# FFN tiles of 432 tokens for the last three batches, and a last output tile in three parts, in an attention + ReGLU kernel

## The chip, the cores and the metric

One core of a Trainium2 chip. The metric is the device time of one execution in microseconds. A verdict compares runs of the two kernels made on the same chip. "Ratio" is the mean time of one kernel's fast runs over that of the other's of the same rounds, so it is not quite the ratio of the medians, and the brackets after it are a 95% interval.

Engines in the profile: PE is TensorE's matmuls, PEld its weight loads, DVE is VectorE, ACT ScalarE, POOL GpSimd, SP SyncE; a q behind the name (SPq) means its instruction queue, for SyncE the issuing of DMAs.

## The reference

```python
# q, k, v: (8, 8, 576, 64); beacon_k, beacon_v: (8, 8, 16, 64)
k_all = concat([beacon_k, k]); v_all = concat([beacon_v, v])       # 592 keys
scores = q @ k_all.T / 8, causal over k, beacons always seen
attn   = softmax(scores) @ v_all                                   # 8 batches x 576 rows
x      = attn laid out as (4608 tokens, 512)
out    = (relu(x @ w_gate) * (x @ w_val)) @ w_out                  # d_ff = 1536
```

## The kernel before: the parts that matter

One stream of matmuls on TensorE mixes the attention of batch b with FFN work on rows of earlier batches. The FFN comes in pieces: `ffn_up(m0, mn, nf)` makes 128 hidden features for `mn` tokens (8 matmuls), `ffn_down` makes 128 rows of the output (12 matmuls of 512 columns). The tiles of tokens are two per batch:

```python
tiles = []
for b in range(B):
    tiles += [(b * S, 368), (b * S + 368, 208)]
```

368 rows are ready when the first group of a batch's queries is through, the other 208 after the second. A pacing rule, run when the program is built, decides how many FFN pieces follow each attention step:

```python
def budget(s):
    best = W0 if s < 8 else CAP * widths[s]
    for r in sorted(set(ready.values())):       # positions at which a tile becomes ready
        if r > pos[s]:
            best = min(best, sum(c for c, _, e in ffn if ready[e] < r) / (r - pos[s]) * widths[s])
    return best
```

So the FFN work that can be done before the next tile is ready is spread evenly until then. Keys and queries of batches 2 to 7 come in five row blocks per batch. SyncE loads each into a staging buffer, GpSimd casts it, and SyncE transposes the block of keys and that of queries by DMA (two transposes for each block).

```python
pieces += [(b, x) for x in (kq[0], vv[0], kq[1], kq[2], vv[1], kq[3], kq[4], vv[2])]
...
def load(t, n, x):
    def go():
        x.issue()                                # DMA from SyncE
        at(t + CD, n - 99, lambda: x.cast(G))    # two positions later
        if x.kind == "kq":
            at(t + TD, n - 99, x.turn)           # three positions later: 2 DMA transposes from SyncE
```

These calls are placed by position in the stream, but each engine works off its own list in order. The attention output is also transposed by DMA from SyncE (`x_turn`, tile `xT`). SyncE's list thus holds loads, key transposes and output transposes, in one order.

The first score matmuls of a batch read key blocks 2 and 0 and query rows 0 to 367, which lie in query blocks 0, 1 and 2: all of the first three blocks are needed at once.

Of the kernel before, what the change touches and what calls it, by code (L numbers as in the profile page):

```python
# [10 lines left out]
FP32 = mybir.dt.float32  # L11
# [131 lines left out]
def kernel(  # L143
# [12 lines left out]
    nc = tc.nc  # L156
    B, H, S, D = q.shape
    Nb = beacon_k.shape[2]
    P = 128
    d_model = H * D  # L160
    n_tokens = B * S
    d_ff = moe_w_gate.shape[1]
    KM, NF = d_model // P, d_ff // P
    NP = H // 2
# [8 lines left out]
    V, G, A, T = nc.vector, nc.gpsimd, nc.scalar, nc.tensor  # L173

    const = ctx.enter_context(tc.tile_pool(name="const", bufs=1))
    ident = const.tile([P, P], BF16, name="ident")
# [4 lines left out]
    wo = const.tile([P, NF, d_model], BF16, name="wo")  # L181
# [9 lines left out]
    stage = main.enter_context(tc.tile_pool(name="stage", bufs=NSTG))  # L191
# [24 lines left out]
    class Load:  # L216
# [41 lines left out]
        def cast(self, *engs):  # L258
            Load.open -= 1
            eng = engs[0]  # L260
            cp = eng.copy if eng is A else eng.tensor_copy
            if self.kind == "v":
                b, t0, t1 = self.key
                n = KT4 if t0 == NKT - 1 else P
                if n == P and t1 == NKT:
                    cp(vs[b % 2][:n, t0:t1 - 1, :, 0:D], self.st[:n, :1].rearrange("p j (h d) -> p j h d", d=D))
                    cp(vs[b % 2][:KT4, t1 - 1:t1, :, 0:D], self.st[:KT4, 1:2].rearrange("p j (h d) -> p j h d", d=D))
                    return self
                cp(vs[b % 2][:n, t0:t1, :, 0:D],  # L269
                   self.st[:n, :t1 - t0].rearrange("p j (h d) -> p j h d", d=D))  # L270
                return self
            self.c = c16.tile([P, 2, H * D], BF16, name="c16")
            if self.kind == "bk":
                cp(self.c[:Nb, 0], self.st[:Nb, 0])
            elif self.kind == "first":
                dst = self.c.rearrange("p a n -> p (a n)")[:, :12 * D].rearrange("p (r a d) -> p a r d", a=2, d=D)
                src = self.st[:, :, :6 * D].rearrange("p a (r d) -> p a r d", d=D)
                for a, e in enumerate(engs):
                    (e.copy if e is A else e.tensor_copy)(dst[:, a], src[:, a])
            else:  # L280
                n = KT4 if self.key[1] == NKT - 1 else P
                cp(self.c[:n], self.st[:n])  # L282
            return self
# [21 lines left out]
    def direct(c, b, p0, p1, part):  # L305
        r0, r1, _ = PARTS[part]
        for i, src in enumerate((k, q)):
            G.dma_start(c[i * D:(i + 1) * D, 2 * p0:2 * p1, r0 * D:r1 * D], runs(src, b, p0, p1, part))  # L308
# [19 lines left out]
    class Burst:  # L328
        pass

    def qk(u):
        u.s, u.p, u.parts = [], [], []
        kq = kqs[u.b % 2]
        for segs, cols, _ in SLABS[u.g]:
            s = s_ps.tile([P, 2, 512], FP32, name="s")
            for (kt, q0, n, c) in segs:
                for a in range(2):
                    rows = slice(a * D, (a + 1) * D)
                    T.matmul(s[:, a, c:c + n], kq[rows, 0, u.pi, kt * P:(kt + 1) * P],  # L339
                             kq[rows, 1, u.pi, Nb + q0:Nb + q0 + n], start=True, stop=True)  # L340
            u.s.append(s)
# [53 lines left out]
    def av(u):  # L395
        qt = QGROUPS[u.g]
        o = f_ps.tile([P, len(qt), 2, D + 2], FP32, name="f")
        blocks = {}
        for p, segs in u.parts:
            for (kt, q0, n, c) in segs:  # L400
                for j, qi in enumerate(qt):
                    r0, rn = QROWS[qi]
                    if q0 <= r0 and r0 + rn <= q0 + n:
                        blocks[j, kt] = (p, c + r0 - q0)
        first = True
        for j, qi in enumerate(qt):
            kts = sorted(kt for (jj, kt) in blocks if jj == j)
            m = 80 if qi == 4 else P
            for a in range(2):
                for kt in kts:  # L410
                    p, c = blocks[j, kt]
                    kr = P if kt < 4 else KT4
                    T.matmul(o[:m, j, a, 0:D + 1], p[:kr, a, c:c + m],  # L413
                             vs[u.b % 2][:kr, kt, 2 * u.pi + a, 0:D + 1],
                             start=first, stop=(kt == kts[-1]), skip_group_check=True)
                    first = False
        parts = ((0, 3, P),) if u.g == 0 else ((0, 1, P), (1, 2, 80))
        for j0, j1, m in parts:
            i0 = qt[j0]
            r = rall[:m, u.b, u.pi, i0:i0 + j1 - j0]  # L420
            V.reciprocal(r, o[:m, j0:j1, :, D])  # L421
            V.tensor_mul(  # L422
                u.x[:m, i0:i0 + j1 - j0, u.pi * P:(u.pi + 1) * P].rearrange("p j (a d) -> p j a d", a=2),
                o[:m, j0:j1, :, 0:D], r.unsqueeze(3).to_broadcast([m, j1 - j0, 2, D]))
# [15 lines left out]
    hbs = {}  # L440
# [25 lines left out]
    def ffn_down(i, ms):  # L466
        rows = slice(i * HB + ms * P, i * HB + (ms + 1) * P)

        def last(mid=None):
            for n0 in (0, 256):  # L470
                o = f_ps.tile([P, 256], FP32, name="f")
                for nf in range(NF):
                    T.matmul(o, hbs[i][:, nf, ms * P:(ms + 1) * P], wo[:, nf, n0:n0 + 256],  # L473
                             start=(nf == 0), stop=(nf == NF - 1))
                ob = osb_p.tile([P, 256], FP32, name="ob")
                A.copy(ob, o)
                (A if n0 else nc.sync).dma_start(out[rows, n0:n0 + 256], ob)

        if (i + 1) * HB == n_tokens and ms == HB // P - 1:
            return last  # L480

        def go(mid=None):
            o = f_ps.tile([P, d_model], FP32, name="f")
            for nf in range(NF):
                T.matmul(o, hbs[i][:, nf, ms * P:(ms + 1) * P], wo[:, nf, :],  # L485
                         start=(nf == 0), stop=(nf == NF - 1))
            if mid:
                mid()
            ob = osb_p.tile([P, d_model], FP32, name="ob")
            A.copy(ob, o)  # L490
            oq = nc.sync if len(ffn) < 8 else OQ
            oq.dma_start(out[rows], ob)  # L492
        return go
# [16 lines left out]

    OQ = G
    NA, PRE = 2, 16
    tiles = []
    for b in range(B):
        tiles += [(b * S, 368), (b * S + 368, 208)]

    with tc.manual_schedule():
        V.memset(ones, 1.0)
# [12 lines left out]
        for b in range(B):  # L531
            for p, g in [(p, g) for g in range(2) for p in range(NP)]:
                u = Burst()
                u.b, u.pi, u.g, u.last, u.parts = b, p, g, p == NP - 1, []
                bursts.append(u)

        def start(u):
# [10 lines left out]
        def chunk(n0, n1):  # L548
            wload(wg, moe_w_gate, n0, n1)
            wload(wv, moe_w_val, n0, n1)  # L550
# [2 lines left out]
        VA = (V.tensor_copy, A.copy)  # L553
        def scores(u):
            start(u)
            qk(u)
            softmax(u)

        first.issue()
# [5 lines left out]
        for p in range(1, NP):  # L565
# [3 lines left out]
        G.affine_select(out=tri[:, :, P:], in_=tri[:, :, P:], pattern=[[0, 2], [1, 240 - P]],  # L569
                        compare_op=ALU.is_ge, fill=0.0, base=Nb, channel_multiplier=-1)  # L570

        first.cast(V, A)
        bk[0].cast(A)
        pair_turn(first, 0, 0, 0, VA)
# [2 lines left out]
        g0 = bursts[:NP]  # L577
        scores(g0[0])
        mask(g0[0], True)
        chunk(0, 256)  # L580
        pair_turn(c0, 0, 2, 0, VV)
        scores(g0[1])
        vl[0][0].cast(G)
# [4 lines left out]
        scores(g0[3])  # L588
        mask(g0[2])
        av(g0[0])  # L590
        direct(c0, 0, 0, NP, 1)
        vl[0][2].issue(lambda ap: G.memset(ap, 0.0))
        bk[1].issue()
        mask(g0[3], True)
        chunk(256, 512)
        av(g0[1])
        av(g0[2])
        x_turn_pair(g0[0], A.copy)
        av(g0[3])
        for u in g0[1:]:  # L600
            x_turn_pair(u, A.copy)
        chunk(512, 1024)
        vl[0][2].cast(G)
        chunk(1024, 1536)
        bk[1].cast(G)
        for j in range(0, NF, 4):
            G.dma_start(wo[:, j:j + 4], moe_w_out[j * P:(j + 4) * P].rearrange("(j p) n -> p j n", p=P))
# [9 lines left out]
        def next_ffn(mid=None):  # L617
            ffn.pop(0)[1](mid)
# [8 lines left out]
        n0 = NF + 2  # L627
# [6 lines left out]
        for p in range(NP):  # L634
            if p < NP - 1:
                pair_turn(c0, 0, p + 1, 1, VV)
            scores(g1[p])
            if p:
                av(g1[p - 1])
            mask(g1[p])  # L640
            next_ffn()
            if p > 1:
                x_turn_pair(g1[p - 2], V.tensor_copy)
        next_ffn()
# [73 lines left out]
        def at(t, n, f):  # L718
            clock.append((t, n, f))
            clock.sort(key=lambda c: c[:2])  # L720

        def load(t, n, x):
            def go():
                x.issue()
                at(t + CD, n - 99, lambda: x.cast(G))
                if x.kind == "kq":
                    at(t + TD, n - 99, x.turn)
            at(t, n, go)

        for b in range(2, B):  # L730
            for i, (_, x) in enumerate([o for o in pieces if o[0] == b]):
                load(pos[enters[b]] - {2: 9.5, 3: 9}.get(b, BB) + i, 8 * b + i, x)

        spent, want = 0.0, 0.0
        for s, e in enumerate(steps):
            units = [u for u in last if last[u] == s - 1]
            want += budget(s)

# [121 lines left out]
```

## Time and profile before

| | before |
|---|---|
| median (range) of the first 3 runs | 378.83 us (377.79 to 378.88) |
| span of the profiled run | 374.2 us |
| TensorE / ScalarE / VectorE / GpSimd busy | 96 / 55 / 51 / 24 % |
| granted TensorE clock | 0.992 |

TensorE is the engine to read: the others have free time nearly everywhere. Its busy share counts overlapping, modelled intervals. I therefore use the time from one matmul's start to the next, less its columns divided by 2.4 GHz: what is left over, about 2.5 ns each, is overhead, a wait, or a slower clock. The prediction shows the lines.

### The profile page before, as it was taken

What the parts mean: (1) busy time and instruction counts of PE and PEld (TensorE: products, weight loads), DVE (VectorE), ACT (ScalarE), POOL (GpSimd) and SP (SyncE); (2) the same over time, 40 slices, a digit from 0 to 9 for tenths busy, and PEclk for the clock granted to TensorE, in tenths of its full rate; (3) what the DMA queues carried; (4) which work ended last, traced back from release to release, by engine and by line L of the source; (5) the groups of instructions that cost most, each with busy time, mean ns of one, the idle gap of its engine ahead of it and who ended that gap; (6) DMA issues with size and microseconds to landing.
All of it is one profiled execution on the core that took longest, in us unless ns stands there. A gap on an engine that the chain in (4) does not pass through costs nothing.

```text
span 374.2 us, 9583 instructions
## 1 busy us (share of the span) xinstructions
PE 358.1 (96%) x3739; PEld 240.4 (64%) x3757; DVE 190.5 (51%) x630; ACT 204.5 (55%) x388; POOL 89.6 (24%) x126
## 2 busy tenths in 40 slices
PE   3889999999999999999999999999999999999995
PEld 2657666567756686565596657865596657865763
DVE  3547357457635663464365645564565625561220
ACT  5655367656555565465466655655565736632321
POOL 6952043231242221411422223120321011000100
PEclk9989999999999999999999999999999999999998
DMA  8999999999999986984869989677674112101202
GB/s 147 181 201 207 204 210 186 200 208 125 182 205 207 163 157 145 218 158 85 203 131 158 140 183 218 132 156 151 156 136 86 25 57 70 30 16 38 86 30 90
DMA packets 156947, 53.12 MB, mean 142 GB/s; under 512 B 146528, under 2 KB 154464, under 8 KB 156896
## 3 DMA queue, kind: packets, MB, share of 16 engines
q1 hardware_dynamic: 145232, 36.85, 55.9%
q0 software_dynamic: 11376, 15.27, 19.3%
q8 instruction: 31, 0.51, 0.6%
q10 hardware_dynamic: 288, 0.33, 0.3%
q14 instruction: 20, 0.16, 0.2%
HBM read 38.47 MB, written 9.44 MB: 128 GB/s over the span
## 4 chain that ended last, share of the span: by engine, by line
PE 90%; DMA 5%; ACT 1%; POOL 1%; issue 1%; DVE 0%; SPq 0%; ACTq 0%; POOLq 0%; DVEq 0%
PE f L454 25%; PE f L446 24%; PE f L485 24%; PE f L413 9%; PE s L356 3%; PE f L356 2%; DMA wv<-in_moe_w_val_dram 2%; DMA stg<-in_v_dram 2%; PE s L339 1%; DMA stg<-in_q_dram 1%; PE f L473 1%; PE f L322 0%; DVE hT L462 0%; ACT p L381 0%; POOL cs L308 0%
## 5 line engine op out<-in xcount | busy, mean ns | idle before, releaser
L462 DVE TENSOR_TENSOR hT<-g,f 128x208 bf16<-128x208 f32 (+14 forms) x288 | 92.7, 351 | 85.8 <-PE f L454 55.2
L454 PE MATMUL f<-xT,wv 128*128 128x368 bf16 (+1 forms) x768 | 126.2, 287 | 1.3 <-DVE hT L462 0.6
L446 PE MATMUL f<-xT,wg 128*128 128x368 bf16 (+1 forms) x768 | 125.8, 286 | 0.7 <-ACT g L449 0.5
L449 ACT ACTIVATE g<-f 128x368 f32<-128x368 f32 (+1 forms) x192 | 78.9, 413 | 78.1 <-PE f L446 37.9
L485 PE MATMUL f<-wo,hT 128*128 128x512 bf16 x402 | 93.6, 379 | 1.0
L454 PEld LDWEIGHTS <-wv 128*128 128x128 bf16 x768 | 71.0, 98 | 27.1 <-issue 1.4
L446 PEld LDWEIGHTS <-wg 128*128 128x128 bf16 x768 | 69.6, 98 | 21.8 <-issue 1.7
L485 PEld LDWEIGHTS <-hT 128*128 128x128 bf16 x420 | 39.9, 98 | 44.2
L490 ACT COPY ob<-f 128x512 f32<-128x512 f32 x35 | 20.5, 585 | 65.0 <-PE f L485 55.7
L365 ACT ACTIVATE p<-s 128x992 bf16<-128x992 f32 (+2 forms) x56 | 53.8, 966 | 0.0
L492 POOL DMA_DIRECT2D out_dram<-ob x32 | 17.3, 542 | 140.0 <-ACT ob L490 130.8
L282 POOL CAST c<-stg 128x1024 bf16<-128x1024 f32 (+1 forms) x30 | 31.3, 1043 | 81.0 <-DMA stg<-in_q_dram 78.4
L421 DVE RECIPROCAL rall<-f 128x2 f32<-128x2 f32 (+1 forms) x96 | 16.6, 173 | 64.1 <-PE f L413 63.7
L413 PEld LDWEIGHTS <-p 128*128 128x128 bf16 (+2 forms) x960 | 38.7, 108 | 10.1 <-issue 6.6
L413 PE MATMUL f<-vx,p 128*128 128x65 bf16 (+2 forms) x960 | 43.8, 200 | 0.1
L422 DVE TENSOR_TENSOR x<-f,rall 128x128 bf16<-128x128 f32 (+1 forms) x96 | 36.3, 378 | 3.5
L363 ACT ACTIVATE p<-f 128x496 bf16<-128x496 f32 (+2 forms) x56 | 28.7, 567 | 7.6 <-PE f L356 7.6
L372 DVE TENSOR_TENSOR p<-p,tri 128x160 bf16<-128x160 bf16 (+1 forms) x72 | 30.4, 424 | 0.5 <-ACT p L365 0.5
L381 ACT ACTIVATE p<-s 128x992 bf16<-128x992 f32 (+2 forms) x32 | 26.1, 865 | 6.1 <-PE s L339 5.9
L269 POOL CAST vx<-stg 128x1024 bf16<-128x1024 f32 (+2 forms) x21 | 18.9, 901 | 29.7 <-DMA stg<-in_v_dram 12.1
L356 PEld LDWEIGHTS <-kq 64*128 64x128 bf16 x384 | 13.8, 94 | 9.7 <-issue 8.1
L356 PE MATMUL s<-kq 64*128 64x208 bf16 (+4 forms) x256 | 16.0, 250 | 0.0
(58 smaller groups left out, 106.8 us busy)
## 6 DMA issues: line engine op xcount, KB each, us to landing
out_dram<-ob POOLq DMA_DIRECT2D x32, 256.0 KB, 3.1
stg<-in_v_dram SPq DMA_DIRECT2D x24, 256.0 KB, 5.1
stg<-in_k_dram SPq DMA_DIRECT2D x18, 256.0 KB, 3.6
stg<-in_q_dram SPq DMA_DIRECT2D x18, 256.0 KB, 4.7
stg<-in_v_dram SPq DMA_DIRECT2D x8, 224.0 KB, 4.4
wo<-in_moe_w_out_dram POOLq DMA_DIRECT2D x3, 512.0 KB, 14.3
stg<-in_k_dram SPq DMA_DIRECT2D x6, 224.0 KB, 3.6
stg<-in_q_dram SPq DMA_DIRECT2D x6, 224.0 KB, 4.7
```

Source lines behind the costliest of these rows:

```text
L282: cp(self.c[:n], self.st[:n])
L356: T.matmul(o[:, c:c + n], kq[rows, 0, u.pi, kt * P:(kt + 1) * P], kq[rows, 1, u.pi, Nb + q0:Nb + q0 + n], start=True, stop=True)
L363: A.activation(p[:, a, :self.cols], self.s[a][:, :self.cols], AF.Exp, scale=scale)
L365: A.activation(p[:, :, :self.cols], self.s[:, :, :self.cols], AF.Exp, scale=scale)
L372: V.tensor_mul(self.p[:, :, :m], self.p[:, :, :m], tri[:, :, :m])
L413: T.matmul(o[:m, j, a, 0:D + 1], p[:kr, a, c:c + m], vs[u.b % 2][:kr, kt, 2 * u.pi + a, 0:D + 1], start=first, stop=(kt == kts[-1]), skip_ ...
L422: V.tensor_mul(u.x[:m, i0:i0 + j1 - j0, u.pi * P:(u.pi + 1) * P].rearrange("p j (a d) -> p j a d", a=2), o[:m, j0:j1, :, 0:D], r.unsqueeze ...
L446: T.matmul(g[:, :mn], wg[:, ki, nf * P:(nf + 1) * P], xT[:, ki, m0:m0 + mn], start=(ki == 0), stop=(ki == KM - 1))
L449: A.activation(gs[:, :mn], g[:, :mn], AF.Relu)
L454: T.matmul(u[:, :mn], wv[:, ki, nf * P:(nf + 1) * P], xT[:, ki, m0:m0 + mn], start=(ki == 0), stop=(ki == KM - 1))
L462: V.tensor_mul(hbs[i][:, nf, c - i * HB:e - i * HB], gs[:, c - m0:e - m0], u[:, c - m0:e - m0])
L485: T.matmul(o, hbs[i][:, nf, ms * P:(ms + 1) * P], wo[:, nf, :], start=(nf == 0), stop=(nf == NF - 1))
```

## The change

Its intent: fewer, wider matmuls for the same columns, and a shorter way from the last matmul to the end.

```diff
     tiles = []
-    for b in range(B):
+    WB = 5
+    for b in range(WB):
         tiles += [(b * S, 368), (b * S + 368, 208)]
+    while tiles[-1][0] + tiles[-1][1] < n_tokens:
+        m0 = tiles[-1][0] + tiles[-1][1]
+        n = -(-(n_tokens - m0) // 512)
+        tiles.append((m0, -(-(n_tokens - m0) // (16 * n)) * 16))     # 4 x 432
```

```diff
         def last(mid=None):
-            for n0 in (0, 256):
-                o = f_ps.tile([P, 256], FP32, name="f")
+            whole = stage.tile([P, 2, H * D], FP32, name="stg")
+            for n0, n, cp, q_ in ((0, 256, A.copy, nc.sync), (256, 128, A.copy, A), (384, 128, V.tensor_copy, nc.sync)):
+                o = f_ps.tile([P, n], FP32, name="f")
   ...           # 12 matmuls
-                ob = osb_p.tile([P, 256], FP32, name="ob")
-                A.copy(ob, o)
-                (A if n0 else nc.sync).dma_start(out[rows, n0:n0 + 256], ob)
+                ob = whole[:, 0, n0:n0 + n]
+                cp(ob, o)
+                q_.dma_start(out[rows, n0:n0 + n], ob)
```

The rest (cut) is hooks at zero, constants that repeat the old values, assertions, and one PSUM buffer that is taken early and never written, which turns the ring of four by one.

More of the change, by code (lines that the diff above doesn't have):

```diff
@@ L329, with keep_busy, qk @@
         pass
-    def qk(u):
+    def keep_busy(ps, n):
+        for _ in range(n):
+            T.matmul(ps[:, :P], ident, ident, start=True, stop=True)
+    def qk(u, idle=0):
         u.s, u.p, u.parts = [], [], []
@@ L335, in qk @@
             s = s_ps.tile([P, 2, 512], FP32, name="s")
+            if not u.s:
+                keep_busy(s[:, 0], idle)
             for (kt, q0, n, c) in segs:
@@ L404, in av @@
                         blocks[j, kt] = (p, c + r0 - q0)
-        first = True
+        first = u.done = True
         for j, qi in enumerate(qt):
@@ L469, in last @@
         def last(mid=None):
-            for n0 in (0, 256):
-                o = f_ps.tile([P, 256], FP32, name="f")
+            whole = stage.tile([P, 2, H * D], FP32, name="stg")
+            for n0, n, cp, q_ in ((0, 256, A.copy, nc.sync), (256, 128, A.copy, A), (384, 128, V.tensor_copy, nc.sync)):
+                o = f_ps.tile([P, n], FP32, name="f")
                 for nf in range(NF):
-                    T.matmul(o, hbs[i][:, nf, ms * P:(ms + 1) * P], wo[:, nf, n0:n0 + 256],
+                    T.matmul(o, hbs[i][:, nf, ms * P:(ms + 1) * P], wo[:, nf, n0:n0 + n],
                              start=(nf == 0), stop=(nf == NF - 1))
-                ob = osb_p.tile([P, 256], FP32, name="ob")
-                A.copy(ob, o)
-                (A if n0 else nc.sync).dma_start(out[rows, n0:n0 + 256], ob)
+                ob = whole[:, 0, n0:n0 + n]
+                cp(ob, o)
+                q_.dma_start(out[rows, n0:n0 + n], ob)
         if (i + 1) * HB == n_tokens and ms == HB // P - 1:
@@ L512 @@
     NA, PRE = 2, 16
+    ORD = 0
+    F0, F1, F3 = 0, 0, 0
+    C1, C2, C3 = 256, 512, 1024
     tiles = []
-    for b in range(B):
+    WB = 5
+    for b in range(WB):
         tiles += [(b * S, 368), (b * S + 368, 208)]
+    while tiles[-1][0] + tiles[-1][1] < n_tokens:
+        m0 = tiles[-1][0] + tiles[-1][1]
+        n = -(-(n_tokens - m0) // 512)
+        tiles.append((m0, -(-(n_tokens - m0) // (16 * n)) * 16))
     with tc.manual_schedule():
@@ L533 @@
                 u = Burst()
-                u.b, u.pi, u.g, u.last, u.parts = b, p, g, p == NP - 1, []
+                u.b, u.pi, u.g, u.last, u.parts, u.done = b, p, g, p == NP - 1, [], False
                 bursts.append(u)
@@ L555, in scores @@
             start(u)
-            qk(u)
+            qk(u, (F1 if u.pi else 0) if u.g == 0 else F3)
             softmax(u)
@@ L570 @@
                         compare_op=ALU.is_ge, fill=0.0, base=Nb, channel_multiplier=-1)
+        keep_busy(f_ps.tile([P, 512], FP32, name="f"), F0)
         first.cast(V, A)
@@ L579 @@
         mask(g0[0], True)
-        chunk(0, 256)
+        chunk(0, C1)
         pair_turn(c0, 0, 2, 0, VV)
@@ L590 @@
         av(g0[0])
-        direct(c0, 0, 0, NP, 1)
+        if ORD == 0:
+            direct(c0, 0, 0, NP, 1)
+        else:
+            chunk(C1, C2)
         vl[0][2].issue(lambda ap: G.memset(ap, 0.0))
@@ L594 @@
         mask(g0[3], True)
-        chunk(256, 512)
+        if ORD:
+            direct(c0, 0, 0, NP, 1)
+        elif C1 < C2:
+            chunk(C1, C2)
         av(g0[1])
@@ L601 @@
             x_turn_pair(u, A.copy)
-        chunk(512, 1024)
+        chunk(C2, C3)
         vl[0][2].cast(G)
-        chunk(1024, 1536)
+        chunk(C3, 1536)
         bk[1].cast(G)
@@ L640 @@
             mask(g1[p])
-            next_ffn()
+            if p or NA < 4:
+                next_ffn()
             if p > 1:
@@ L724, in go, with cast, turn @@
                 x.issue()
-                at(t + CD, n - 99, lambda: x.cast(G))
+                at(t + CD, n - 99, cast)
                 if x.kind == "kq":
-                    at(t + TD, n - 99, x.turn)
+                    at(t + TD, n - 99, turn)
+            def cast():
+                assert x.kind == "kq" or all(u.done for u in bursts if u.b == x.key[0] - 2)
+                x.cast(G)
+            def turn():
+                assert all(u in last and last[u] <= now[0] for u in bursts if u.b == x.key[0] - 2 and u.b)
+                x.turn()
             at(t, n, go)
@@ L732 @@
                 load(pos[enters[b]] - {2: 9.5, 3: 9}.get(b, BB) + i, 8 * b + i, x)
-        spent, want = 0.0, 0.0
+        spent, want, now = 0.0, 0.0, [0]
         for s, e in enumerate(steps):
+            now[0] = s
             units = [u for u in last if last[u] == s - 1]
```

## The prediction

> **What bounds the kernel now.** I read the page first (busy table, slices), then the table by stretches of time, the groups by shape, the waits of TensorE, and last the timeline of the end and of SyncE's DMA queue.
>
> ```profile
> PE 358.1 (96%) x3739; PEld 240.4 (64%) x3757; DVE 190.5 (51%) x630; ACT 204.5 (55%) x388; POOL 89.6 (24%) x126
> ...
> 60.00:100.00 40.00, 39.37 (x443) 27.54 (x445) 24.46 (x83) 25.69 (x49) 11.05 (x12) 1.00 1.04 168
> 100.00:140.00 40.00, 39.89 (x393) 26.55 (x391) 21.31 (x71) 23.82 (x45) 11.04 (x13) 1.00 1.05 188
> 140.00:180.00 40.00, 39.84 (x368) 23.87 (x370) 18.73 (x66) 21.88 (x39) 8.46 (x11) 1.00 0.78 156
> ...
> 312.00:340.00 28.00, 28.00 (x312) 21.48 (x313) 16.91 (x62) 14.85 (x32) 0.54 (x1) 1.00 0.14 33
> 350.00:360.00 10.00, 9.64 (x101) 8.96 (x101) 5.54 (x16) 4.60 (x13) 0.54 (x1) 1.00 0.10 38
> ```
>
> The columns of the stretches are length, then busy time of TensorE, weight loads, VectorE, ScalarE and GpSimd, then granted clock, DMA share and GB/s. From 60 us to the end TensorE is busy all but a few tenths in every 40 us, at clock 1.00; ScalarE and VectorE lie near 55 to 60%. So nothing but TensorE's own time, and whatever makes it wait, can move the end. Busy time alone does not show whether its matmuls run at their floor, so I use spacing from start to start:
>
> ```profile
> 330.43 0.62 PE f L454 x4
> 331.05 0.62 PE f L446 x4
> ...
> 355.60 0.36 PEld L446 LDWEIGHTS <-wg 128*128 128x128 bf16 x4
> 355.69 0.52 PE L446 MATMUL f<-xT,wg 128*128 128x208 bf16 x4
> 355.96 0.10 PEld L454 LDWEIGHTS <-wv 128*128 128x128 bf16 x1
> 356.11 0.64 DVE L462 TENSOR_TENSOR hT<-g,f 128x208 bf16<-128x208 f32 x2
> 356.52 0.52 PE L454 MATMUL f<-xT,wv 128*128 128x208 bf16 x4 [0.31 <-DVE hT L462]
> ...
> 357.79 0.52 PE L446 MATMUL f<-xT,wg 128*128 128x208 bf16 x4
> 358.50 0.52 PE L446 MATMUL f<-xT,wg 128*128 128x208 bf16 x4
> ```
>
> The chain of waits gives four matmuls of 368 columns 0.62 us, 156 ns each to the next start. In the timeline of the last narrow tile eight matmuls of 208 lie between 357.79 and 358.50, so 89 ns each. At 355.69 one narrow group is held up: the next starts at 356.52 instead of 356.05, because VectorE was doing the range check and gave the PSUM buffer back late.
>
> **What the Trainium skill says.** "TensorE: Matmul & The Clock Gate", section "Wait — 56ns, not 53.3ns?", gives a warm spacing of N/2.4 plus about 2.5 ns. The trace agrees: 208 columns give 86.7 + 2.3, 368 give 153.3 + 2.7. Its section "What's actually happening" says that an idle window of about 3.4 us halves the clock; here the stretch 24 to 28 us, just after a 7 us wait for weights, has a granted clock of 0.62 and no later stretch before 360 us has one below 1.00. "DMA: Bandwidth & Descriptors", section "Issuing engines are not separate DMA queues", says that issuing on several engines saves only the sequencers' time, which is usually small. For this kernel's SyncE that time is not small: 1.2 us or more per transpose (below). For the last tile I expect it small.
>
> **The change, part by part.** The calls for filling TensorE have a count of 0; the other constants repeat the old order; one PSUM buffer is taken and never written, which only turns the ring of four by one place. What is real is two things.
>
> (1) Tiles. Batches 5 to 7 had six tiles (368 and 208, three times), now four of 432, the same 1728 columns. Each tile costs 12 x 8 up-projection matmuls, so 576 become 384. Before: 12 x 8 x 3 x (156 + 89) ns = 70.56 us. After: 12 x 8 x 4 x (180 + 2.6) ns = 70.12 us. Saved: 0.44 us, on the path. The down projection is unchanged.
>
> Bubbles of the narrow tiles in those batches: comparing starts with the floor I find 0.48 us (above), 0.29 us near 272.7, and three of 0.08 us, together 1.0 us. Four PSUM buffers cover 4 x 0.36 = 1.4 us with narrow tiles and 4 x 0.73 = 2.9 us with wide ones, while the range check takes 1.3 us, so I take nearly all of it as saved.
>
> ScalarE loses 24 ReLU: 36 x (0.480 + 0.346) = 29.7 us become 48 x 0.533 (480 ns plus 64 columns at the slope of 0.84 ns) = 25.6 us. VectorE loses 24 products (108 to 84 with the cuts at the 512-row blocks), about 24 x 0.15 = 3.6 us. Both engines have slack, so neither counts.
>
> (2) Last output tile. Two halves of 256 become 256 + 128 + 128. TensorE: 24 x 109 = 2.62 us before, 12 x 109 + 24 x 56 = 2.65 us after. The last copy falls from 0.37 us (ScalarE, 256 columns) to about 0.25 (VectorE; 128 columns in its products take 0.28). The last store is 64 KB instead of 128 KB, which landed after 1.8 us; I give it 0.1. Together 0.2 us saved.
>
> Sum of the direct gains: 0.44 + 1.0 + 0.2 = 1.6 us.
>
> (3) What moves. The pacing rule of the kernel deals FFN pieces out over the attention steps so that all that is ready is used up just before the next tile becomes ready. The tile of batch 5 now ends at row 432 of 576, so it waits for the second query group instead of the first. I stepped the rule through for both tile lists. The pieces are spread more thinly over batches 2 to 5: the step before batch 2 has 3.8 us of FFN instead of 5.1, the four steps from there to batch 3 have 25.5 us instead of 28.1; after the last attention step 43.0 us of FFN are left instead of 30.9. TensorE's total is the same, but it comes to batch 3 about 3.9 us sooner, to batch 5 some 11 us. Its keys and queries must be there sooner too.
>
> **Rivals.** First rival: SyncE becomes the bound at the start of batch 3.
>
> ```profile
> 96.85 1.47 SPq L254 DMA_DIRECT2D stg<-in_k_dram  x1
> 98.37 0.58 SPq L255 DMA_DIRECT2D stg<-in_q_dram  x1
> 98.99 1.63 SPq L244 DMA_DIRECT2D stg<-in_v_dram  x2
> 100.73 3.16 SPq L296 DMA_TRANSPOSE kq<-c  x2
> 103.94 0.58 SPq L254 DMA_DIRECT2D stg<-in_k_dram  x1
> 104.56 0.58 SPq L255 DMA_DIRECT2D stg<-in_q_dram  x1
> 105.24 5.20 SPq L429 DMA_TRANSPOSE xT<-x  x3
> 110.55 2.53 SPq L296 DMA_TRANSPOSE kq<-c  x2
> ...
> 115.67 0.55 PE L356 MATMUL s<-kq 64*128 64x208 bf16 x8
> ```
>
> The queue of SyncE (SPq) issues back to back here, with no gaps over 0.5 us from 76 to 142 us. The pair at 110.55 transposes the third key tile of batch 3, which its first score matmuls need; its second transfer lands at 115.06, and those matmuls start at 115.8: a slack of 0.7 us. If TensorE comes 3.9 us sooner and the queue cannot, it waits 3.2 us, less the 0.8 us for which the queue itself waited on TensorE's and VectorE's work at 105.24: about 2.4 us. That loses more than all the gains. For batches 5 and 6 the same slack (5.5 and 3.4 us by the median of 3.3 us from issue to landing) shrinks by 4.6 and about 2.2 us, so there it is nearly gone: another 0.4 us expected. For it: the solid queue. Against it: several long issues (1.5 to 2 us) contain waits that may shift too. A wait over 3.4 us could halve the clock as at 24 us and cost 1.7 us more. Outcome if it comes in full: 378.8 - 1.6 + 2.8 = 380.0.
>
> Second rival: queue and loads shift along, nothing waits; outcome 377.2. For it: the tile list has a new number (5 batches keep their own tiles) which at 8 would give the old list back, so somebody probably measured and kept 5.
>
> Third rival: steps with only two down blocks of FFN (5.2 us, now three among batches 2 to 5) leave TensorE too little beside three exponentials. Attention adds about 2 us of matmuls to such a step and ScalarE needs 3 x 1.0 + 2 x 0.58 = 4.2 us, so it should stay TensorE-bound; at most 0.3 us each.
>
> **Range and chances.** Between 377.2 and 380.0 I give the wait a little more than a third of its size on average, because of the sign that the number was tuned: 378.2 us. The spread of runs is 1.1 us, the wait may be 0 to 4 us: 375.7 to 380.8. Two per cent is 7.6 us; nothing in the sum comes near it: faster 0.01, within 0.98, slower 0.01.
>
> **What would show it.** Up-projection rows of 432 columns, 384 in all, spaced 182 to 183 ns; no wait of TensorE on VectorE's product in the last tile; the tail after the last attention matmul longer by about 12 us. For the first rival: the waits of TensorE list the score matmuls behind a transfer into the key tile, near 112 us, of 2 to 3 us; for the second, they don't. I am wrong if the even tiles are spaced wider than 185 ns, if the wait exceeds 5 us, or if the end moves by more than half a microsecond because of the last tile.

## The result, and the profile after

| | before | after |
|---|---|---|
| median, 6 runs each | 378.54 us | 389.88 us |
| range | 376.88 to 380.44 | 387.29 to 391.03 |
| span of the profiled run | 374.2 us | 389.2 us |
| granted clock of the runs with the change | – | 0.977 to 0.995 |

Ratio 1.0285 [1.0237, 1.0332]: slower, where I had foretold 378.2 us. First the page of the changed kernel, TensorE's busy time and the clock in 40 slices:

```profile
PE 362.8 (93%) x3577; PEld 226.2 (58%) x3577; DVE 189.5 (49%) x607; ACT 201.2 (52%) x364; POOL 89.9 (23%) x126
...
PEclk9999999999997999999999996999999999999998
```

Fewer matmuls (the profile of before lacks 18 records of the down projection, so the counts differ by 162 instead of 180), yet more busy time, and two dips of the clock in the middle. Next, the waits of TensorE in the changed kernel (total us, times, longest):

```profile
PE s L363 <- DMA kq<-c: 7.7, 2, 4.9
```

This line did not exist before. It is the score matmuls waiting for transposed keys, twice. Where and why shows in the timeline of SyncE's queue beside the first score matmuls of batches 3 and 6. Batch 3 in the changed kernel (before is in the prediction: 105.24, 110.55, 115.67):

```profile
106.14 5.27 SPq L436 DMA_TRANSPOSE xT<-x  x3
...
111.52 2.53 SPq L296 DMA_TRANSPOSE kq<-c  x2
112.81 0.39 PE L363 MATMUL f<-kq 64*128 64x80 bf16 x6
113.04 0.34 PE L363 MATMUL s<-kq 64*128 64x208 bf16 x4
...
116.23 0.62 PE L363 MATMUL s<-kq 64*128 64x128 bf16 x4 [2.85 <-DMA kq<-c]
```

Batch 6, before:

```profile
226.65 5.28 SPq L429 DMA_TRANSPOSE xT<-x  x3
...
232.04 2.51 SPq L296 DMA_TRANSPOSE kq<-c  x2
...
239.62 0.39 PE L356 MATMUL f<-kq 64*128 64x80 bf16 x6
239.85 0.55 PE L356 MATMUL s<-kq 64*128 64x208 bf16 x8
```

and after:

```profile
225.37 5.22 SPq L436 DMA_TRANSPOSE xT<-x  x3
...
230.71 2.63 SPq L296 DMA_TRANSPOSE kq<-c  x2
...
231.38 0.34 PE L363 MATMUL s<-kq 64*128 64x208 bf16 x4
...
236.59 0.62 PE L363 MATMUL s<-kq 64*128 64x128 bf16 x4 [4.87 <-DMA kq<-c]
```

Compare clock times, not order. SyncE issues the pair of key transposes at 110.6 and 232.0 before, at 111.5 and 230.7 after: hardly moved. TensorE reaches the batch at 115.7 and 239.9 before, at 113.0 and 231.4 after. It comes up to 8.5 us sooner to keys that come when they always came.

What the waits cost beyond themselves shows in the stretches just behind them (columns as in the prediction; the clock is the third figure from the right):

```profile
119.00:123.00 4.00, 4.00 (x30) 2.58 (x29) 1.51 (x6) 1.45 (x3) 1.74 (x3) 0.56 0.76 198
236.50:242.00 5.50, 5.41 (x31) 2.67 (x32) 0.97 (x5) 0.00 (x0) 1.65 (x2) 0.50 0.97 167
```

TensorE is fully busy there at half its clock: from 115.7 to 122.5 and from 235.1 to 242.0 by the trace's clock records, 6.8 us each.

The sum, by starts of matmuls against columns / 2.4 GHz: between 112.5 and 125 us the changed kernel has 5.9 us over the floor, between 231 and 243 us it has 7.4; before has none at these places. Of the 13.3 us, 3.0 + 5.0 are the two waits and the remaining 5.3 the halved clock. From the end of the last copy to the end of the span it is 5.5 us after and 4.0 before, 1.5 us more. That is 14.8 of the 15.0 us between the two traces; the gains and the rest of the run (before had one half-clock stretch early, from 23.6 to 27.0 us, this run had not) balance to near zero in it.

Two traces are two executions, and these two lie at opposite ends: the traced run of before took 376.06 us, less than any of its six runs in the table, and that of after 391.03, the most of its six. Between the medians it is 11.3 us. The clock is part of that spread: the runs of after at 387.29 and 387.43 us had a granted clock of 0.995 and 0.991, the traced one 0.978.

### The profile page after: what moved, and what is told of

It is laid out like the page before. It is cut to its first block, busy times and chain, and to the rows that moved or that the text cites. A ratio compares the mean times of both kernels' runs of the same rounds, so it can differ in the third digit from the quotient of the medians.

```text
span 389.2 us, 9150 instructions
## 1 busy us (share of the span) xinstructions
PE 362.8 (93%) x3577; PEld 226.2 (58%) x3577; DVE 189.5 (49%) x607; ACT 201.2 (52%) x364; POOL 89.9 (23%) x126
## 4 chain that ended last, share of the span: by engine, by line
PE 73%; DMA 10%; SPq 8%; POOL 3%; DVE 2%; issue 2%; ACT 1%; POOLq 0%; DVEq 0%; ACTq 0%
PE f L461 20%; PE f L453 20%; PE f L493 18%; PE f L420 7%; DMA stg<-in_q_dram 4%; SPq L296 4%; PE s L363 2%; DMA kq<-c 2%; DMA wv<-in_moe_w_val_dram 2%; PE f L363 2%; DMA cs<-in_q_dram 2%; PE s L346 1%; SPq L244 1%; SPq L436 1%; POOL c L282 1%
## 5 line engine op out<-in xcount | busy, mean ns | idle before, releaser
L469 DVE TENSOR_TENSOR hT<-g,f 128x368 bf16<-128x368 f32 (+16 forms) x264 | 89.0, 369 | 91.0 <-PE f L461 76.4
L461 PE MATMUL f<-xT,wv 128*128 128x368 bf16 (+2 forms) x672 | 122.1, 304 | 2.4 <-DVE hT L469 1.8
L453 PE MATMUL f<-xT,wg 128*128 128x368 bf16 (+2 forms) x672 | 122.7, 305 | 0.6 <-ACT g L456 0.5
L456 ACT ACTIVATE g<-f 128x368 f32<-128x368 f32 (+2 forms) x168 | 74.7, 448 | 84.9 <-PE f L453 39.1
L493 PE MATMUL f<-wo,hT 128*128 128x512 bf16 x420 | 96.6, 384 | 0.2
L461 PEld LDWEIGHTS <-wv 128*128 128x128 bf16 x672 | 63.2, 98 | 36.1 <-DVE hT L469 2.3
L453 PEld LDWEIGHTS <-wg 128*128 128x128 bf16 x672 | 61.5, 98 | 28.4 <-issue 2.1
L420 PEld LDWEIGHTS <-p 128*128 128x128 bf16 (+2 forms) x960 | 39.8, 109 | 11.3 <-issue 7.3
L420 PE MATMUL f<-vx,p 128*128 128x65 bf16 (+2 forms) x960 | 44.8, 202 | 0.4 <-DVE p L400 0.3
L379 DVE TENSOR_TENSOR p<-p,tri 128x160 bf16<-128x160 bf16 (+1 forms) x72 | 28.8, 407 | 5.5 <-ACT p L372 5.5
```

What stands on the lines that cost most here:

```text
L379: V.tensor_mul(self.p[:, :, :m], self.p[:, :, :m], tri[:, :, :m])
L420: T.matmul(o[:m, j, a, 0:D + 1], p[:kr, a, c:c + m], vs[u.b % 2][:kr, kt, 2 * u.pi + a, 0:D + 1], start=first, stop=(kt == kts[-1]), skip_ ...
L453: T.matmul(g[:, :mn], wg[:, ki, nf * P:(nf + 1) * P], xT[:, ki, m0:m0 + mn], start=(ki == 0), stop=(ki == KM - 1))
L456: A.activation(gs[:, :mn], g[:, :mn], AF.Relu)
L461: T.matmul(u[:, :mn], wv[:, ki, nf * P:(nf + 1) * P], xT[:, ki, m0:m0 + mn], start=(ki == 0), stop=(ki == KM - 1))
L469: V.tensor_mul(hbs[i][:, nf, c - i * HB:e - i * HB], gs[:, c - m0:e - m0], u[:, c - m0:e - m0])
```

## The experiments

Theory A: the even tiles make the rule spread the FFN more thinly over batches 2 to 5, so TensorE outruns the loading of keys and queries, and the idle waits halve its clock. Rival B: the tile shape itself costs (PSUM buffers held longer, thinner spread). Theory C: the new last tile lengthens the end. Fifteen runs.

**1. Old tiles, new last tile.** Edit to the changed kernel: `WB = 5` becomes `WB = 8`.

> The changed kernel with the six old tiles, so only the last output tile (and the turn of the PSUM ring) is new. Theory A (the even tiles let TensorE run ahead of its keys): no wait on key tiles, no halved clock around 115 or 235 us, so nearly the time of before. Theory C (the end got longer: the last matmuls are narrower, so TensorE's branch starts later, and VectorE's branch now comes last too): 1.3 to 1.8 us over before, about 380.2, with 5.4 to 5.6 us from the end of the last copy to the end of the span instead of 4.0. My prediction's own figure for the last tile: 0.2 us under before.

Measured: 379.74 against 379.80 us, ratio 1.0001 [0.9978, 1.0024]; one wait on keys of 0.7 us, no half clock in mid-run. With the old tiles the slowdown is gone, so the tiles carry it. (Its trace also has a wait of 1.6 us on transposed x at 112 us; it matters below.) The end of the trace is long as expected (5.6 us from last copy to end), but the total is not: theory C's 1.5 us is missing. My own 0.2 us under before can't be told from zero here.

**2. Third block loaded sooner.**

```diff
-(kq[0], vv[0], kq[1], kq[2], vv[1], ...)
+(kq[0], kq[2], vv[0], kq[1], vv[1], ...)
```

> The changed kernel whole, with one line changed: the load of the third key tile of each batch from 2 on is issued second instead of fourth, some 10 us sooner. Theory A: the two waits of 3.0 and 4.9 us are gone and with them the halved clock: 390 - 8 - 5 = 377, at most 1.5 us over before. Rival B (the tile shape itself, through PSUM buffers or the thinner spread of FFN pieces, costs the time and the waits are a symptom): 386 or more, waits turned up at other places.

Measured: 390.16 us, ratio 1.0266 [1.0238, 1.0294]. A miss, and mine, not the theory's. The profile of this run:

```profile
111.67 3.27 SPq L296 DMA_TRANSPOSE kq<-c  x2
...
116.66 0.49 PE L363 MATMUL s<-kq 64*128 64x368 bf16 x2 [4.17 <-DMA kq<-c]
```

The wait has moved from the matmul of 128 columns (key block 2) to that of 368, whose queries span blocks 0 to 2. I had only exchanged which of the three needed blocks came last. The run serves as a second copy of the slow kernel, on the chip of runs 1 to 8.

**3. The same reorder in the kernel before.**

> The kernel before, with the same one-line reorder. Theory A: it had 0.6 us of slack at batch 3 and over 2 us elsewhere, no waits to remove, so within 1 us of before. If it gains over 2 us, the reorder does something that the theory does not know, and the run third_key_sooner says less.

Measured: 379.88 us, ratio 1.0021 [0.9993, 1.005]: no change, as expected.

**4. Waits filled with work.** Dummy matmuls on the identity before the first scores of batches 3 and 6, overwritten by the scores; the keys come no sooner. The edit, with its first lines cut:

```diff
+                if sl is slabs[14 * (u0.b - 2)] and u0.b in FILL:      # FILL = {3: 54, 6: 90}
+                    keep_busy(s_[0] if isinstance(s_, list) else s_[:, 0], FILL[u0.b])
                 sl.qk(s_)
```

> The changed kernel with 54 matmuls of 128 columns on the identity before the first score matmuls of batch 3 and 90 before those of batch 6 (3.0 and 5.0 us of work, overwritten right after): the keys come no sooner, but TensorE does not stand idle. If the idle waits are what halves the clock: no half-clock stretch near 115 and 235 us, 3.4 to 6.8 us less than the changed kernel, about 384. If the clock falls for another reason: unchanged, about 390.

Measured: 385.77 us, ratio 1.0173 [1.0142, 1.0204], 4.4 us less than run 2 in the same rounds. Its stretches behind the two places:

```profile
117.00:123.00 6.00, 6.00 (x68) 4.08 (x67) 4.37 (x14) 2.98 (x6) 2.13 (x3) 1.00 1.29 175
235.00:242.00 7.00, 6.95 (x66) 4.16 (x64) 1.99 (x10) 2.07 (x4) 2.39 (x3) 1.00 1.12 162
```

The clock is 1.00 where it was 0.5. So it was the idleness that halved the clock at these two places, and this part is 4 to 5 us of the loss. Useless work made the kernel faster; the rest, the late keys, stays.

**5. All three blocks loaded before the values.**

```diff
-(kq[0], vv[0], kq[1], kq[2], vv[1], ...)
+(kq[0], kq[1], kq[2], vv[0], vv[1], ...)
```

> The changed kernel with all three key and query tiles that a batch's first scores read loaded before the value tile (order key 0, 1, 2, then value), which also puts the third pair of key transposes ahead of the output transposes of the batch before. The run third_key_sooner only exchanged which of the three came last. Theory A (TensorE runs ahead of its keys and queries): the waits at batches 3 and 6 fall from 3.0 and 4.9 us to under 1 us, no halved clock there: 390 - 8 - 5 = 377 to 380. Rival B (the tile shape or the thinner spread itself costs): 386 or more although the waits on key tiles are gone.

Measured: 381.57 us, ratio 1.0048 [1.0029, 1.0068]. The view of waits no longer lists key tiles at all; its largest new line is

```profile
PE f L453 <- DMA xT<-x: 1.5, 1, 1.5
```

That wait, at batch 3, is not in the trace of the changed kernel. The key transposes now go ahead of those of x: the latter are issued at 111.9 us instead of 106.1. But this order alone does not make the wait, for run 1 has one of 1.6 us there with the old order. Of a loss of 2.85% some 2.4% are gone with one line, and the 432-token tiles are still there. Rival B falls. The time is a little over the range that I wrote. Its trace has a half clock from 23.8 to 30.7 us, before the reordered loads begin, twice as long as that of before; whether this is the reason is not shown.

**6. Value loads from GpSimd.** For batches 2 to 7 the value loads are issued on GpSimd's queue.

> The changed kernel with the value loads of batches 2 to 7 issued by GpSimd instead of SyncE: 3 to 5 us less issue time on SyncE's queue for each batch, the same bytes on the same 16 DMA engines. If the issue time of SyncE sets when the keys land (theory A1): the waits shrink by at least 2 us each, 380 to 384. If the DMA engines' own time sets it (rival A2): waits within 1 us of 3.0 and 4.9, 388 to 391.

Measured: 383.19 us median, one of the six runs slow, ratio of the fast runs 1.0047 [1.0012, 1.0083]; these five spread from 380.17 to 384.54. The waits on keys fall to one of 1.3 us, at the second query group of batch 5. But this is no clean test of issue time against DMA time: in its trace TensorE was late itself at batch 3 (a wait of 2.2 us on x at 73 us and a half-clock stretch behind it), and SyncE stood still for 3.4 us (103.3 to 106.7) before it could transpose x. It fits the theory and proves no part of it.

**7. Uneven tiles.** 368, 464, 448, 448: as few matmuls, but the first is ready after the first query group again.

> The changed kernel with four tiles of 368, 464, 448 and 448 tokens in place of 432 four times: as few matmuls, but the first needs only the first query group of batch 5, so the pacing rule spreads less thinly: TensorE comes to batch 3 by 1.2 us sooner than before instead of 3.8, to batch 6 by 7.7 us instead of 15. Theory A: at batch 3 a wait of under 1 us, at batch 6 one of 2.5 to 4.5 us, clock halved there at most: 383 to 387. Rival B1 (the number and width of the tiles costs): as the changed kernel, 389 to 391.

Measured: 378.36 us, ratio 0.9975 [0.9933, 1.0016]. Better than I expected: at batch 3 waits of 1.6 us on keys and 2.1 on x, at batch 6 none, no half clock in mid-run. My figure for batch 6 was too high: there SyncE's pair of key transposes came at 228.7, TensorE at 235. Wide tiles do no harm that shows here; when the first one becomes ready does.

**8. The new last tile alone, in the kernel before.**

> The kernel before with nothing but the new last output tile in three parts, without the turn of the PSUM ring. Theory C: 1.3 to 1.7 us over before (from the end of the last copy to the end of the span 5.4 to 5.6 us instead of 4.0). My prediction: 0.2 us under before. The run old_tiles had the long end but no longer time, so if this one is longer, the turn of the ring gave back about 1.5 us there.

Measured: 379.19 us, ratio 0.9994 [0.9964, 1.0023].

**9. Keys first, with the old last tile.**

> The run keys_first with the last output tile as it was before (two halves of 256, both copied by ScalarE). Theory C (the new end is 1.5 us longer in every trace): from the end of the last copy to the end of the span 4.0 us instead of 5.3, and 1.5 us less time than keys_first, about 380.0. Rival (the last tile is neutral in the total, as old_tiles and before_new_last had it): within 0.7 us of keys_first.

Measured: 377.88 us, ratio 0.997 [0.9928, 1.0012], on another chip, one run of six slow. That is 0.8% under run 5, more than theory C allows; but the clock was 1.000 in four of these runs and 0.987 to 0.992 in all of run 5, so the pair does not isolate the last tile. Its trace, one of its slower runs (380.54 us), has a wait of 3.9 us on x at batch 3 and a half clock from 117.9 to 121.3 us.

**10. Uneven tiles, keys first, old last tile.**

> Four tiles of 368, 464, 448 and 448, keys and queries loaded ahead of the value tile, the last output tile as before. Theory A: no waits on key tiles at all, so this shows the gain of fewer matmuls and bubbles that the prediction put at 1.4 us: 377.5 to 379, ratio 0.993 to 0.998. If the wide tiles gave nothing: 379.8.

Measured: 380.98 us, ratio 1.0072 [1.003, 1.0115]. A miss: no waits on keys, but one of 4.8 us on transposed x at 112 us and a half-clock stretch behind it. Run 11 has such a wait too, with the old tiles; how much of it is the reorder's comes after run 15.

**11. Keys first in the kernel before.**

> The kernel before with keys and queries loaded ahead of the value tile and nothing else. Theory A: there was no wait on keys, so the time of before within 1 us; a wait of 1 to 2 us on a transposed x tile may come in, as in keys_first, since the key transposes now go ahead of those of x. If it is over 1.5 us faster or slower, the reorder has an effect of its own which must be taken off keys_first.

Measured: 380.09 us, ratio 1.0064 [1.0019, 1.0109], over the 1 us that I allowed, with this wait in its profile and a half clock from 114.4 to 117.8 us behind it:

```profile
PE f L446 <- DMA xT<-x: 3.2, 1, 3.2
```

The reorder seems to have a price of its own, 0.6% with an interval from 0.2 to 1.1%; the wait is not proof of it (after run 15). With the same order of loads, the changed kernel stands at 1.0048 and the kernel before at 1.0064, each against the plain kernel before on its own chip: no loss from the change is left that these intervals would show.

**12. Keys first for batches 4 to 7 only**, even tiles.

> The changed kernel with keys and queries loaded ahead of the value tile for batches 4 to 7 only; batch 3 keeps the old order. Theory A: the wait of 3 us at batch 3 stays (with a half-clock stretch after it in some runs), that of 5 us at batch 6 and its half-clock stretch go: 7 to 8.5 us less than the changed kernel, ratio to before 1.005 to 1.012. If batch 6's wait was only a consequence of batch 3's: it stays, ratio 1.025.

Measured: 383.07 us, ratio 1.0111 [1.0078, 1.0143]. The wait at batch 3 stays (2.7 us), this time with no half clock behind it; that at batch 6 and its half-clock stretch are gone. In their place stands a wait of 1.8 us on x at 246.5 us with a half clock from 248.0 to 251.5. So at least some 1.7% of the 2.85 belonged to batch 6, and 1.1% is left for batch 3, this new wait and whatever else remains.

**13 to 15.** Uneven tiles with the old last tile; the same with the values of batches 2 and 3 loaded by GpSimd; run 8 once more.

> Four tiles of 368, 464, 448 and 448, the last output tile as before. uneven_tiles was at 0.9975 of before with 1.6 us of wait on keys and 2.1 on x at batch 3. If the end is in the total (theory C): 1.5 us less, ratio 0.990 to 0.995. If not: 0.9955 to 1.0.

> As uneven_old_last, with the value loads of batches 2 and 3 issued by GpSimd, which takes some 3 us of issue time off SyncE's queue between 76 and 112 us, where it is full. Theory A1 (SyncE's queue sets the pace): the two waits at batch 3 shrink to under 1 us together, 2 to 3.5 us less than uneven_old_last, ratio 0.985 to 0.992. If the DMA engines' time sets it: no gain, or a loss.

> The kernel before with only the new last output tile, once more, now with runs of before in the same rounds. Theory C: ratio 1.003 to 1.005 (1.3 to 1.7 us). If the time lost at the end is not in the total: 0.998 to 1.002.

Measured: 378.24 us, ratio 0.9999 [0.997, 1.0028]; 378.07 us, ratio 0.9971 [0.9944, 0.9999]; 380.40 us, ratio 1.0026 [0.9995, 1.0056]. The second misses what I wrote for theory A1: the waits at batch 3 are gone, but a wait of 2.9 us on x at 70 us took their place, with a half clock from 71.9 to 78.7. None of these beats the kernel before by an amount worth the name; the best interval ends at 0.9999.

Run 15's trace shows one thing more. Up to the last output tile runs 8 and 15 are the kernel before, with its old order of loads. Yet run 15 has this wait at batch 3 (111.9 to 114.6 us), with a half clock from 114.8 to 118.2 us, and run 8 waits there for 1.1 us on x and 1.0 on keys:

```profile
PE f L446 <- DMA xT<-x: 2.7, 1, 2.7
```

The trace of before that I predicted from has none of this. So the kernel before already runs at the edge at batch 3, where some executions wait and some do not, and a wait on x in one trace of runs 5 and 9 to 11 (1.5 to 4.8 us) cannot be put down to the reorder alone. At batch 6 no trace with the old tiles has such a wait; that one comes with the even tiles.

**The last tile.** In the profile the lines of the last copy are, before and after:

```profile
369.85 0.37 ACT L476 COPY ob<-f 128x256 f32<-128x256 f32 x1 [0.94 <-PE f L473]
```

```profile
383.35 0.29 DVE L484 COPY stg<-f 128x128 f32<-128x128 f32 x1 [9.80 <-PE f L481]
```

The copy is shorter, as foretold. From its end to the end of the span it is 5.3 to 5.6 us in all ten traces with the new last tile and 3.9 to 4.6 in the seven with the old one. In the trace TensorE's sequencer comes to the branch after the kernel some 17 matmuls ahead of the array: 1.8 us before the last matmul starts with 256 columns, 0.9 with 128; the branch record then lasts 3.8 us in both, with a 16 KB instruction fetch inside. VectorE's branch, long past before, now comes last too. The Trainium skill, "Runtime: NRT & Kernel Launch", section "Instruction fetch mechanics", says that a taken branch outside the fetched window forces a fetch of its target; the trace has a fetch at this place, but that this mechanism sets the 1.5 us is argued, not tested. In the totals the 1.5 us (0.4%) does not show: ratios 1.0001, 0.9994 and 1.0026 in the runs that have it alone, of which only the last interval reaches 0.4%. That contradiction stays open.

## Why the prediction was wrong

- **What bounds the kernel, and the direct gains on TensorE:** right in kind. Tiles of 432 came to be 384 matmuls spaced 182.5 ns (0.73 us for four), and TensorE no longer waits behind the range check. No run shows the 1.4 us by itself: uneven tiles came out at 0.9975 and 0.9999, at 0.9971 with the value loads of two batches moved, and at 1.0072 with keys first.
- **The pacing and the first rival:** right in kind. The tail after the last attention matmul grew from 40.8 to 53.4 us, 12.5 against about 12 foretold. At batch 3 TensorE did outrun its keys, with a wait of 2.85 us (3.0 by starts) against 2.4. That this size came so close is luck: TensorE was 2.6 us sooner (115.67 to 113.04), not 3.9, and SyncE's pair was issued 1.0 us later (110.55 to 111.52), not 0.8 sooner. 2.6 - 0.7 + 1.0 gives 2.9 where the prediction has 3.9 - 0.7 - 0.8.
- **The step that failed** is the term for batches 5 and 6, "another 0.4 us expected". Measured: none at the start of batch 5 and 5.0 us at batch 6. I took the slack in the old trace (by a median landing; the actual one, at 237.4, leaves 2.6 us at batch 6 and not 3.4) and subtracted only the shortening of the last stretch (2.2 us), as though SyncE's queue would shift along with TensorE's lead of earlier batches. It did not: the pair for batch 6 was issued at 230.7 against 232.0, while TensorE, even after waiting and a halved clock at batch 3, came 8.5 us sooner. The prediction itself has TensorE some 11 us ahead at batch 5, twice the slack there, and does not use it. For batch 6 the same count gives 15 us.
- **The clock:** I said that only a wait over 3.4 us could halve it, at 1.7 us. A wait of 2.85 us did, and each of the two half-clock stretches lasted 6.8 us: 5.3 us in that trace. Filling the waits gave back 4.4. The old trace had already spoken against my limit, and I misread it. The 7 us "wait for weights" is the transfer in the chain of waits (first line below); TensorE worked on beside it, and itself waited for these weights only 0.53 us (second line). That is the longest of its waits in the 3.4 us before its clock was halved from 23.6 to 27.0 us; the others took 0.45, 0.25 and 0.08:

```profile
16.38 7.15 DMA wv<-in_moe_w_val_dram
...
23.57 1.40 PE L454 MATMUL f<-xT,wv 128*128 128x368 bf16 x4 [0.53 <-DMA wv<-in_moe_w_val_dram]
```

- **The weighting:** I cut the wait to about a third of its size on average because the tile list looked tuned. That is no evidence from a profile; without it my own rival stood at 380.0. With 5.0 us for 0.4, 5.3 for no clock loss and 3.0 for 2.4 the sum becomes 378.8 - 1.6 + 13.3 = 390.5, beside 389.88 measured.
- **The last tile:** its direct parts were right; the 0.2 us gain was not seen: the end is 1.5 us longer in the traces, which is one of the prediction's own signs of being wrong, and nothing is clear in the totals.

Shown: the old tiles, or an order of loads without late keys, take the loss away, and filling the idle waits keeps the clock from being halved there. Not shown: how long a wait must be for that (see the end). Argued only: that issue time in SyncE's queue, rather than the time of the DMAs behind it, holds the keys back. In the chain of waits at batch 6, the changed kernel has both:

```profile
224.69 5.14 DMA stg<-in_q_dram
...
229.98 1.05 POOL c L282
231.03 0.87 SPq L296
...
231.95 4.51 DMA kq<-c
```

The load is issued at 224.69 in both traces, and then takes 12 us through load, cast, transpose and landing. From 189.4 to 247.8 us SyncE's queue in the changed kernel has no gap over 0.44 us, but waits for GpSimd's casts lie hidden within its issues (3.3 us between 180 and 240), so this does not decide it.

## What to carry to other kernels

An engine at 96% can hide a second chain at nearly the same speed. When a change lets the first run ahead, compare its new arrival times with the second chain's clock times, summed from the start, and not with slack in the last stretch. A wait of a few microseconds on TensorE can cost nearly twice its length (here 8.0 us of waits cost 13.3), when the clock halves behind it; and before you move a load forward, list every tile that the first consumer reads and everything the load overtakes. And one trace is one execution: read a slack of under a microsecond from several.

## What the Trainium skill lacked or had wrong

- "TensorE: Matmul & The Clock Gate", section "What's actually happening", has the half clock after at least one idle window of about 3.4 us. Here an idle wait of 2.85 us was enough (half clock from 115.7 to 122.5 us), and one of 2.2 us (run 6, at 73 us), 1.8 us (run 12, at 246.5 us) and even short ones of at most 0.53 us (before, ahead of 23.6 us); waits of 2.1 and 1.6 us 5 us apart in run 7 and one of 2.7 us at batch 3 in run 12 were not. So no length of a wait divides these runs. The half-clock stretches before the end of the run lasted 3.4 or 6.8 us, which agrees with its window.
- "DMA: Bandwidth & Descriptors", section "Issuing engines are not separate DMA queues", calls the issuing time usually small. On SyncE a DMA transpose took 1.18 us at the least and 1.26 in the median to issue, 95 times per run, against a median of 3.3 us from issue to landing; and in the kernel before the queue had a single gap over 0.5 us (0.52, at 95.1) from 76 to 141.3 us.
- "Runtime: NRT & Kernel Launch", section "Instruction fetch mechanics", names the stall at a taken branch without a length. TensorE's branch record at the end lasted 3.8 us in both kernels, and began about 17 matmuls ahead of the last one.
